# Freeing the fill of waits, reordering the half round and spreading the last picks in a convolution and expert-routing kernel

## The chip, the cores and the metric

The kernel runs on one core of one Trainium2 chip. The metric is the device time of one execution in microseconds (us), the lower the better. Each run comes with the mean granted clock of TensorE (1.0 is full speed). A run is called slow when it is over 1.5% above the fastest run of the same kernel on that chip, and slow runs are kept out of all ratios (the medians quoted are of all runs). Some of the experiments landed on two other chips, on which the kernel before took some 18% longer. They are marked, and their absolute times are never set beside those of the ordinary chips.

## The reference

Eight sequences of 3,584 rows of 192 numbers pass through a lightweight convolution (7 taps, causal, one softmaxed filter per group of 24 channels). Each row then goes to one of eight experts, the one with the largest gate logit. The expert is a two-layer network, and its result is scaled by a softmax gate and an output gate.

```python
# x: (8, 3584, 192), weight: (8, 7); cut to what matters
w = softmax(weight)                                  # per head
out = einsum('hk,bskhg->bshg', w, windows_of(x_pad)) # causal convolution
x = out.reshape(28672, 192)
logits = x @ w_gate                                  # (192, 8)
e_idx = argmax(logits, axis=1)
gate_w = softmax(logits)[arange(N), e_idx]
eom = 1 / (1 + exp(-(x @ w_output_gate)))
for e in range(8):
    mask = e_idx == e
    h = maximum(x[mask] @ w1[e], 0.0)                # 192 -> 1024
    ye = h @ w2[e]                                   # 1024 -> 192
    out[mask] = gate_w[mask, None] * eom[mask, e, None] * ye
```

## The kernel before

The 28,672 rows are cut into 16 units of 1,792. For each unit a front part and, later, an expert part run, and the two are interleaved instruction by instruction.

The front of a unit is two generators. `front_a` convolves on TensorE (8 steps), transposes (6 steps), multiplies with the gates and transposes back (2 steps). `front_b` picks the expert of each row, counts rows per expert, computes each row's position (a matmul with a triangular matrix plus one that adds the counts, called the positions matmul below), and permutes the rows into expert order by eight groups of matmuls with 0/1 masks. GpSimd then scatters each group, with computed row addresses, into a buffer in device memory that is sorted by expert.

```python
    def evac(o, i):                  # empties a "pf" accumulation buffer
        sync_flip[0] ^= 1
        if sync_flip[0] or fill[0] is not None:
            nc.scalar.copy(out=o, in_=i)
        else:
            nc.vector.tensor_copy(out=o, in_=i)
    # ... in front_b, after the positions matmul pk:
        nc.vector.tensor_tensor(out=dm[P], in0=pk[P, 0:NB * E]..., in1=msk[P], op=ALU.mult)
        nc.vector.tensor_reduce(out=pos[P], in_=dm[P], axis=AX.X, op=ALU.add)
        # dd, R, dd, dst, du: five operations that make the rows' destinations
        ...
        prep(0)                      # scaled rows and mask of the first permutation group
        prep(1)
    # ...
    def scatter(u, du, xs, i):
        i = nc.gpsimd.indirect_dma_start(out=xcg2, out_offset=...du..., in_=xs...)
        nodep(i, f"sc{u}", [f"sc{v}" for v in range(NU)] + ["load"])
```

The list at the end of `scatter` names the transfers that a scatter need not wait for. The "guards", eight writes of zero rows to the start of each expert's region, are not in it.

The expert part works on slots of 512 sorted rows. A slot has four quarters. The first layer of two quarters (`first`) and the second layer of each (`second`) surround one step of the front of unit u+2, and one of the permutation of unit u+1. Four slots, so 16 quarters, are called a half round here, since in each the slots of four of the eight experts are served.

```python
    load_w(0)
    load_w(1)
    drain(front_a(0))
    for u in range(U0 + 1):                      # the fill: units 0, 1, 2
        fa, fb = front_a(u + 1, u < U0), front_b(u)
        drain(fa, 1)
        while drain(fb, 1):
            drain(fa, 2 if u < U0 else 1)
            emit_in(len(pend))                   # scatters
        if u == 0:
            drain(fa)
            load_w(2)
            load_w(3)
            for e in range(E):                   # the guards
                i = nc.sync.dma_start(out=xcg[e * CAP:e * CAP + TT, :]..., in_=zrow)
                nodep(i, "guard", ())
        # ...
    for u in range(U0, NU):                      # the half rounds
        # ...
            for q in range(4):
                pos = 4 * k + q
                if q % 2 == 0:
                    s.first(q // 2)
                drain(fa, 1)
                if prev is not None:
                    prev.second(q)
                    emit_out()                   # scatters of results
                if pos < 8:
                    drain(fs, 1)
                elif pos < 12:
                    drain(fa, 1)
                else:
                    drain(fbn, 1)
                emit_in(len(pend))
```

In the last unit three further slots of 256 rows are chosen at run time from what is left over. These are the "picks", each a chain of some fifteen small operations on VectorE, which all stand in one block in the middle of the half round before the last unit's (561 to 570 us), where that unit's slots are loaded.

## Time and profile before

| | before |
|---|---|
| time, median of 3 | 647.33 us (646.89 to 647.94) |
| span of the profiled run | 645.5 us, clock 0.981 |
| first slot's first matmul | at 89.18 us |
| half rounds, positions matmul to positions matmul | 37.14 and 38.39 us alternating |
| positions matmul of unit 15 to the end | 101.6 us |

These lines of the page give each engine's busy time, then the granted clock in 40 slices of the span (in tenths, 9 is full), then the chain of work that ended last by engine.

```profile
PE 586.5 (91%) x4544; PEld 360.3 (56%) x4544; DVE 406.3 (63%) x1362; ACT 355.4 (55%) x586; POOL 401.5 (62%) x419
...
PEclk9999859999999999999999999999999999999997
...
PE 66%; DVE 19%; ACT 6%; DMA 4%; issue 3%; SPq 0%; POOL 0%; DVEq 0%; ACTq 0%; POOLq 0%
```

TensorE (PE) is nearly always busy, yet the last chain runs through it for 66% of the span only. In 19% VectorE (DVE) holds it up. The slices with 8 and 5, at about 65 to 97 us, are the fill's end, where TensorE also runs at a lower clock.

### The profile page before, as it was taken

The numbers are of one execution on the slowest core, as the hardware profiler recorded it, in microseconds if no ns is written. First come the engines' busy times: TensorE is split into PE (matmuls) and PEld (weight loads), VectorE is DVE, ScalarE is ACT, GpSimd is POOL, SyncE is SP. The second block draws the span as 40 slices with busy tenths as digits, with TensorE's granted clock in tenths as the row PEclk, the third lists the DMA queues.
The fourth block names the chain that finished last, engine by engine and source line by source line (L and its number), as shares of the span: only waits on it lengthen the run. The fifth ranks groups of instructions, "written<-read, shape, count | busy, mean of one in ns | idle before, by whom it ended". The sixth has DMA issues, their size and how long they took to land.

```text
span 645.5 us, 13578 instructions
## 1 busy us (share of the span) xinstructions
PE 586.5 (91%) x4544; PEld 360.3 (56%) x4544; DVE 406.3 (63%) x1362; ACT 355.4 (55%) x586; POOL 401.5 (62%) x419
## 2 busy tenths in 40 slices
PE   3998739999999999999999999999999999979993
PEld 1554415656665566656566566655566565546662
DVE  7567536584957658494775849577594956943332
ACT  1676525554665555556555555555555565656661
POOL 1362726876775756667476655756566674777773
PEclk9999859999999999999999999999999999999997
DMA  6979439994654647264553637355372525246631
GB/s 160 191 186 258 132 76 201 143 211 137 138 169 117 176 106 171 85 153 131 117 155 101 185 87 165 105 114 165 92 188 88 107 82 113 73 108 136 188 115 37
DMA packets 162569, 88.14 MB, mean 137 GB/s; under 512 B 116765, under 2 KB 153792, under 8 KB 162496
## 3 DMA queue, kind: packets, MB, share of 16 engines
q1 hardware_dynamic: 131872, 43.92, 30.3%
q0 software_dynamic: 29728, 43.30, 25.8%
q8 instruction: 36, 0.59, 0.4%
q14 instruction: 37, 0.30, 0.2%
q10 hardware_dynamic: 896, 0.03, 0.1%
HBM read 35.92 MB, written 43.06 MB: 122 GB/s over the span
## 4 chain that ended last, share of the span: by engine, by line
PE 66%; DVE 19%; ACT 6%; DMA 4%; issue 3%; SPq 0%; POOL 0%; DVEq 0%; ACTq 0%; POOLq 0%
PE pyt L655 18%; PE pp L613 13%; PE pf L290 11%; PE pp L620 8%; PE pf L444 5%; DVE ht L631 5%; PE pf L313 5%; PE pf L304 5%; ACT ht L633 4%; DVE xrow L423 2%; DVE pm L428 2%; DVE cv L280 2%; PE pf L322 2%; DMA out_dram<-y,oi 1%; DMA xt<-in_x_dram 1%
## 5 line engine op out<-in xcount | busy, mean ns | idle before, releaser
L482 POOL DMA_INDIRECT out_dram<-y,oi x246 | 245.6, 998 | 127.6 <-ACT y L661 63.4
L633 ACT ACTIVATE ht<-pp 128x1024 f16<-128x1024 f32 (+1 forms) x189 | 183.1, 1001 | 69.8 <-PE pp L620 67.0
L655 PEld LDWEIGHTS <-ht 128*128 128x128 f16 x1968 | 166.6, 98 | 58.2 <-issue 29.5
L655 PE MATMUL pyt<-wres,ht 128*128 128x192 f16 x1920 | 192.7, 246 | 1.5 <-DVE ht L631 1.5
L462 POOL DMA_INDIRECT xcg_sorted<-xs,du x128 | 131.5, 1027 | 92.2 <-DVE tk L502 22.1
L290 PE MATMUL pf<-xt,band 118*112 118x384 f32 x256 | 109.4, 523 | 19.1 <-DMA xt<-in_x_dram 10.8
L631 DVE TENSOR_SCALAR ht<-pp 128x1024 f16<-128x1024 f32 (+1 forms) x63 | 74.7, 1185 | 71.8 <-PE pp L613 71.8
L661 ACT COPY y<-pyt 128x384 f32<-128x384 f32 x123 | 59.0, 479 | 85.6 <-PE pyt L655 84.1
L613 PE MATMUL pp<-xa,wres 128*128 128x512 f16 x240 | 92.9, 387 | 9.1 <-DMA xa<-xcg_sorted 9.1
L613 PE MATMUL pp<-xb,wres 128*128 128x512 f16 x240 | 91.3, 380 | 1.2 <-DMA xb<-xcg_sorted 1.2
L620 PE MATMUL pp<-xb,wres 64*128 64x512 f16 x240 | 73.0, 383 | 1.6 <-ACT ht L633 1.2
L620 PE MATMUL pp<-xa,wres 64*128 64x512 f16 x240 | 73.0, 383 | 0.0
L444 PE MATMUL pf<-xrow,pm 112*128 112x194 f16 x512 | 65.1, 249 | 5.8 <-DVE pm L428 4.1
L613 PEld LDWEIGHTS <-wres 128*128 128x128 f16 x480 | 34.8, 97 | 60.7 <-issue 59.7
L290 PEld LDWEIGHTS pf<-xt,band 118*112 118x112 f32 x256 | 42.5, 185 | 41.6 <-DVE cv L280 11.5
L278 ACT COPY cv<-pf 112x384 f32<-112x384 f32 x80 | 38.1, 478 | 46.5 <-PE pf L290 38.6
L428 DVE TENSOR_SCALAR pm<-pos,pos 112x256 f16<-112x256 f16 x256 | 62.1, 307 | 0.0
L423 DVE TENSOR_TENSOR xrow<-cv,gs 112x384 f16<-112x384 f32 x121 | 61.9, 551 | 0.0
L444 PEld LDWEIGHTS <-pm 112*128 112x128 f16 x512 | 44.7, 98 | 15.3 <-DVE pm L428 7.7
L304 PE MATMUL pf<-identf,cv 112*128 112x112 f32 x384 | 50.7, 260 | 2.3 <-ACT tt L278 2.1
L278 ACT CAST xs<-pf 128x388 f16<-128x388 f32 x76 | 37.1, 492 | 27.5 <-PE pf L444 27.5
L304 PEld LDWEIGHTS pf<-identf,cv 112*128 112x128 f32 x384 | 40.9, 141 | 10.0 <-ACT tt L278 3.4
(139 smaller groups left out, 447.2 us busy)
## 6 DMA issues: line engine op xcount, KB each, us to landing
xt<-in_x_dram SPq DMA_DIRECT2D x8, 1344.0 KB
xt<-in_x_dram SPq DMA_DIRECT2D x8, 1260.0 KB
out_dram<-y,oi POOLq DMA_INDIRECT x246
wres<-in_moe_w_dram POOLq DMA_DIRECT2D x8, 384.0 KB
wd<-wres SPq DMA_DIRECT2D x3, 768.0 KB
wres<-in_moe_w_dram POOLq DMA_DIRECT2D x8, 256.0 KB
xcg_sorted<-xs,du POOLq DMA_INDIRECT x128
xcg_sorted<-zrow SPq DMA_DIRECT2D x8, 256.0 KB
```

The source lines that it names most:

```text
L278: nc.scalar.copy(out=o, in_=i)
L290: nc.tensor.matmul(pc[0:BT, 0:NB * GH], band[0:KI, h, :], xt[0:KI, :, h * GH:(h + 1) * GH], start=True, stop=True)
L304: nc.tensor.matmul(pt[:, j * BT:(j + 1) * BT], cvf[0:BT, m * 2 * D + i * 128:m * 2 * D + (i + 1) * 128], identf[0:BT, 0:BT], is_transpose= ...
L428: nc.vector.tensor_scalar(out=pms[i][P, l, :], in0=pos16[P], scalar1=pos[P, l * NG + i:l * NG + i + 1], scalar2=None, op0=ALU.is_equal)
L444: nc.tensor.matmul(ps[:, r * XW:(r + 1) * XW], pm[P, l, r * 128:(r + 1) * 128], xr[P, l * NG + i, :], start=(r == 0 and l == 0), stop=(r = ...
L462: i = nc.gpsimd.indirect_dma_start(out=xcg2, out_offset=bass.IndirectOffsetOnAxis(ap=du[:, i:i + 1], axis=0), in_=xs.rearrange("p r w -> p ...
L482: i = nc.gpsimd.indirect_dma_start(out=out, out_offset=bass.IndirectOffsetOnAxis(ap=oi[:, j:j + 1], axis=0), in_=y[:, j, :], in_offset=Non ...
L613: nc.tensor.matmul(pps[r][:, l, :], w[:, o2:o2 + 128], x, start=(r == 0), stop=(r == 1))
L620: nc.tensor.matmul(pps[r][:, l, :], w[p0:p0 + 64, c:c + 128], x[p0:p0 + 64], start=(r == 1), stop=(r == 0))
L631: nc.vector.tensor_relu(out=ht, in_=pps[r])
L633: nc.scalar.activation(out=ht, in_=pps[r], func=AF.Relu)
L655: nc.tensor.matmul(self.pp[:, o:o + D], self.ht[fc // 2][:, fc % 2, q * 128:(q + 1) * 128], self.w[:, w:w + D], start=(fc == 0 and q % 2 = ...
```

## The change

It has three parts. In the fill, scatters no longer wait for the guards, the weights are split into pieces that are issued between scatters, and the order of convolution and permutation steps differs. In the half rounds, the front's steps stand at other quarters, ScalarE and VectorE take fixed shares of the copies, and the destination arithmetic moves behind the first permutation mask. The picks are spread, one after each of the last unit's first three slots.

```diff
-    def load_w(e):              # four transfers of one expert
+    def w_pieces(e):            # the same four, as a list
...
+    wq = deque(p for e in range(E) for p in w_pieces(e))
+    def load_w(n):
+        while n and wq:
+            nc.gpsimd.dma_start(*wq.popleft())
+            n -= 1
...
+    evac_on = [None]
     def evac(o, i):
         sync_flip[0] ^= 1
-        if sync_flip[0] or fill[0] is not None:
+        if evac_on[0] is not None:
+            act = evac_on[0] == "act"
+        else:
+            act = sync_flip[0] or fill[0] is not None
+        if act:
...
-        dd = pr.tile(...)       # the five destination operations
-        ...
         prep(0)
+        dd = pr.tile(...)       # now between the first mask and the second
+        ...
         prep(1)
...
-        nodep(i, f"sc{u}", [f"sc{v}" for v in range(NU)] + ["load"])
+        nodep(i, f"sc{u}", [f"sc{v}" for v in range(NU)] + ["load", "guard"])
...
-            drain(fa, 2 if u < U0 else 1)
+            n += 1
+            drain(fa, 1 if u == U0 or n > 8 else 2 if n < 8 else 0)
             emit_in(len(pend))
+            if u < U0 and n > 4 and n % 2:
+                load_w(1)
...
-        if u == NU - 1:
-            for sel, bap, inv in [pick(TP // 2) for _ in range(ND)]:
-                ...
+    def load_pick():
+        sel, bap, inv = pick(TP // 2)
+        ...
...
+                if 0 <= 16 * (u - U0) + pos - 4 < 16:
+                    load_w(1)
                 if q % 2 == 0:
                     s.first(q // 2)
-                drain(fa, 1)
+                if pos in (0, 2, 4, 6, 8, 10, 12):
+                    evac_on[0] = "act" if pos < 8 else None
+                    drain(fa, 1)
+                if pos == 14:
+                    drain(fbn, 1)
                 if prev is not None:
                     prev.second(q)
                     emit_out()
+                if pos in (1, 3, 5, 7, 8, 9, 10, 11):
+                    evac_on[0] = "dve" if pos < 8 else None
+                    drain(fa, 2 if pos == 9 else 1)
                 if pos < 8:
+                    evac_on[0] = "act"
                     drain(fs, 1)
...
+                if pos == 12:
+                    drain(fbn, 1)
+                if pos == 15:
+                    drain(fbn, 2)
...
+                if u == NU - 1 and q == 3 and k < ND:
+                    todo.append(load_pick())
```

More of the change, by code (lines that the diff above doesn't have):

```diff
@@ L202 @@
     wres = const.tile([128, E * WE], FP16)
-    def load_w(e):
+    def w_pieces(e):
         o = e * WE
         w = moe_w1[e]
-        nc.gpsimd.dma_start(
-            wres[:, o:o + F].rearrange("p (l c) -> p l c", l=2),
-            bass.AP(tensor=w.tensor, offset=w.offset,
-                    ap=[[F, 128], [64 * F + F // 2, 2], [1, F // 2]]))
-        nc.gpsimd.dma_start(wres[0:64, o + F:o + WA], w[0:64, F // 2:F])
-        nc.gpsimd.dma_start(wres[64:128, o + F:o + WA], w[128:D, 0:F // 2])
-        nc.gpsimd.dma_start(
-            wres[:, o + WA:o + WE].rearrange("p (c d) -> p c d", d=D),
-            moe_w2[e].rearrange("(c p) d -> p c d", p=128))
+        return [
+            (wres[:, o:o + F].rearrange("p (l c) -> p l c", l=2),
+             bass.AP(tensor=w.tensor, offset=w.offset,
+                     ap=[[F, 128], [64 * F + F // 2, 2], [1, F // 2]])),
+            (wres[0:64, o + F:o + WA], w[0:64, F // 2:F]),
+            (wres[64:128, o + F:o + WA], w[128:D, 0:F // 2]),
+            (wres[:, o + WA:o + WE].rearrange("p (c d) -> p c d", d=D),
+             moe_w2[e].rearrange("(c p) d -> p c d", p=128))]
+    wq = deque(p for e in range(E) for p in w_pieces(e))
[3 more added lines that the diff above has]
+            n -= 1
     GE = NG * E
@@ L393, in front_b @@
         nc.vector.tensor_reduce(out=pos[P], in_=dm[P], axis=AX.X, op=ALU.add)
-        dd = pr.tile([128, NG, E + 1], FP32, tag="dd", name="dd")
-        nc.vector.tensor_tensor(
-            out=dd, in0=pk[:, c0 + NSEG:c0 + 2 * NSEG].rearrange("p (i e) -> p i e", e=E + 1),
-            in1=bass.AP(tensor=R9.tensor, offset=R9.offset,
-                        ap=[list(R9.ap[0]), [0, NG], [1, E + 1]]), op=ALU.add)
-        nc.vector.tensor_tensor(out=R, in0=R, in1=pk[:, c0 + 2 * NSEG:NK], op=ALU.add)
-        nc.vector.scalar_tensor_tensor(
-            out=dd, in0=pk[:, c0:c0 + NSEG].rearrange("p (i e) -> p i e", e=E + 1),
-            scalar=rowf[:, 0:1], in1=dd, op0=ALU.is_le, op1=ALU.mult)
-        dst = pr.tile([128, NG], FP32, tag="dst", name="dst")
-        nc.vector.tensor_reduce(out=dst, in_=dd, axis=AX.X, op=ALU.max)
-        du = pr.tile([128, NG], U32, tag="du", name="du")
-        nc.vector.tensor_scalar(out=du, in0=dst, scalar1=rowf[:, 0:1], scalar2=None, op0=ALU.add)
         xr = xrows[u % 2]
@@ L432, in front_b @@
         prep(0)
+        dd = pr.tile([128, NG, E + 1], FP32, tag="dd", name="dd")
+        nc.vector.tensor_tensor(
+            out=dd, in0=pk[:, c0 + NSEG:c0 + 2 * NSEG].rearrange("p (i e) -> p i e", e=E + 1),
+            in1=bass.AP(tensor=R9.tensor, offset=R9.offset,
+                        ap=[list(R9.ap[0]), [0, NG], [1, E + 1]]), op=ALU.add)
+        nc.vector.tensor_tensor(out=R, in0=R, in1=pk[:, c0 + 2 * NSEG:NK], op=ALU.add)
+        nc.vector.scalar_tensor_tensor(
+            out=dd, in0=pk[:, c0:c0 + NSEG].rearrange("p (i e) -> p i e", e=E + 1),
+            scalar=rowf[:, 0:1], in1=dd, op0=ALU.is_le, op1=ALU.mult)
+        dst = pr.tile([128, NG], FP32, tag="dst", name="dst")
+        nc.vector.tensor_reduce(out=dst, in_=dd, axis=AX.X, op=ALU.max)
+        du = pr.tile([128, NG], U32, tag="du", name="du")
+        nc.vector.tensor_scalar(out=du, in0=dst, scalar1=rowf[:, 0:1], scalar2=None, op0=ALU.add)
         prep(1)
@@ L682, in chain @@
             yield from g
-    load_w(0)
-    load_w(1)
+    load_w(8)
     drain(front_a(0))
@@ L690 @@
         drain(fa, 1)
+        n = 0
         while drain(fb, 1):
-            drain(fa, 2 if u < U0 else 1)
+            n += 1
+            drain(fa, 1 if u == U0 or n > 8 else 2 if n < 8 else 0)
             emit_in(len(pend))
+            if u < U0 and n > 4 and n % 2:
+                load_w(1)
+        if u < U0:
+            drain(fa)
         if u == 0:
-            drain(fa)
-            load_w(2)
-            load_w(3)
             for e in range(E):
                 i = nc.sync.dma_start(
-                    out=xcg[e * CAP:e * CAP + TT, :].rearrange("(p g) w -> p (g w)", g=GR), in_=zrow)
+                    out=xcg[e * CAP:e * CAP + TT, :].rearrange("(p g) w -> p (g w)", g=GR),
+                    in_=zrow)
                 nodep(i, "guard", ())
-        elif u < U0:
-            drain(fa)
     def loads(u):
@@ L709, in loads @@
             todo.append((wres[:, e * WE:(e + 1) * WE], inv, slot_load(base, u)))
-        if u == NU - 1:
-            for sel, bap, inv in [pick(TP // 2) for _ in range(ND)]:
-                base = reg(bap[0:1, 0:1], [ET.SP], E * CAP - TT)
-                todo.append((w_dyn(sel), inv, slot_load(base, u, TT // 2)))
-        return todo
+        return todo
+    def load_pick():
+        sel, bap, inv = pick(TP // 2)
+        base = reg(bap[0:1, 0:1], [ET.SP], E * CAP - TT)
+        return w_dyn(sel), inv, slot_load(base, NU - 1, TT // 2)
     todo = loads(U0)
@@ L729 @@
             fa, fbn = front_a(u + 2), front_b(u + 2)
-        nxt = None
-        for k, (w, inv, xabi) in enumerate(todo):
-            if 0 < 4 * (u - U0) + k <= EH:
-                load_w(EH - 1 + 4 * (u - U0) + k)
+        k = 0
+        while k < len(todo):
+            w, inv, xabi = todo[k]
             s = Slot(xabi, w, inv)
@@ L742 @@
                     emit_out()
+                if pos in (1, 3, 5, 7, 8, 9, 10, 11):
+                    evac_on[0] = "dve" if pos < 8 else None
+                    drain(fa, 2 if pos == 9 else 1)
                 if pos < 8:
+                    evac_on[0] = "act"
                     drain(fs, 1)
-                elif pos < 12:
-                    drain(fa, 1)
-                else:
+                    evac_on[0] = None
+                    emit_in(len(pend))
+                if pos == 12:
                     drain(fbn, 1)
-                emit_in(len(pend))
+                if pos == 15:
+                    drain(fbn, 2)
                 if pos == 7 and u + 1 < NU:
                     nxt = loads(u + 1)
+                if u == NU - 1 and q == 3 and k < ND:
+                    todo.append(load_pick())
             prev = s
+            k += 1
         todo = nxt
```

## The prediction

> **What bounds the kernel now.** I read the page first, for the stages, then the timelines of the engines in each stage. TensorE is busy 91% of the span and carries 66% of the chain of waits, so a gain has to come out of TensorE's idle time or its slow clock. There are three places: the fill (0 to 89 us), the steady half rounds, and the tail. The fill first: TensorE's timeline (start, us, engine, line, tiles, idle before and what ended it).
>
> ```profile
> 80.34 0.23 PE L386 MATMUL pf<-lsum,np 64*128 64x152 f16 x1
> 89.18 0.59 PE L613 MATMUL pp<-xa,wres 128*128 128x512 f16 x1 [8.61 <-DMA xa<-xcg_sorted]
> 90.51 0.59 PE L613 MATMUL pp<-xb,wres 128*128 128x512 f16 x1 [0.74 <-DMA xb<-xcg_sorted]
> ...
> 97.09 0.38 PE L613 MATMUL pp<-xb,wres 128*128 128x512 f16 x1
> ```
>
> The first slot's matmuls wait 8.61 us for their rows, then run at 0.59 us instead of 0.38. The rows are loaded only when the last scatter of unit 2 has landed, so GpSimd's timeline tells why they are late:
>
> ```profile
> 49.74 0.98 POOL L213 DMA_DIRECT2D wres<-in_moe_w_dram  x1
> 63.26 1.05 POOL L462 DMA_INDIRECT xcg_sorted<-xs,du  x1 [12.54 <-DVE du L407]
> 64.61 1.38 POOL L462 DMA_INDIRECT xcg_sorted<-xs,du  x1 [0.30 <-issue]
> ...
> 83.83 0.98 POOL L462 DMA_INDIRECT xcg_sorted<-xs,du  x1 [0.31 <-issue]
> ```
>
> GpSimd stands idle for 12.54 us with unit 1's first tile ready since 49.7 (its copy on ScalarE starts at 49.18 and takes 0.50), then issues 16 scatters back to back, one per 1.29 us. The releaser named, du, is unlikely: unit 1's du was written at 47.30. In the instruction order of the kernel before, this scatter also waits on all eight hardware queues, which are the guard writes (issued from 46.78 to 53.84). I take the guards for the cause.
>
> The steady half round: TensorE's waits over two half rounds (196.57 to 272.11 us), then where they lie in the first of them.
>
> ```profile
> PE pf L290 <- DVE cv L280: 1.1, 2, 0.7
> PE pf L313 <- DVE tt L280: 0.4, 1, 0.4
> PE pf L304 <- ACT tt L278: 0.3, 1, 0.3
> ```
>
> ```profile
> 213.53 0.90 PE L290 MATMUL pf<-xt,band 118*112 118x384 f32 x2 [0.74 <-DVE cv L280]
> ...
> 233.14 1.71 PE L313 MATMUL pf<-tt,wg 128*32 128x448 f32 x16 [0.41 <-DVE tt L280]
> ```
>
> These show only 1.8 us of 75.5, because short waits vanish under the modelled ends of matmuls. Start-to-start times show more. Unstalled pieces are: two quarters of a slot 2.83 us (598.97 to 601.80, first and second layer), a convolution step 0.65, a transpose step 0.39, the gate matmuls 1.65, their transposes 0.48, a permutation group 0.335, the counts 0.15 and the positions 0.40. A half round is 8x2.83 + 8x0.65 + 6x0.39 + 1.65 + 0.48 + 8x0.335 + 0.55 = 35.5 us. The trace has 75.54/2 = 37.77. So 2.25 us per half round is waiting, nearly all for the two "pf" buffers to be emptied. At 212.93 VectorE empties one that was full since about 211.8 (its matmuls start at 210.98 and take 0.81), because a 1.22 us relu and the 1.41 us plan stand before it in its queue:
>
> ```profile
> 211.31 0.17 DVE L518 TENSOR_SCALAR iu<-iv 128x16 uint32<-128x16 f32 x1
> 211.40 0.48 DVE L428 TENSOR_SCALAR pm<-pos,pos 112x256 f16<-112x256 f16 x2
> 211.79 1.22 DVE L631 TENSOR_SCALAR ht<-pp 128x1024 f16<-128x1024 f32 x1
> 212.93 0.55 DVE L280 COPY cv<-pf 112x384 f32<-112x384 f32 x1
> ```
>
> The tail: TensorE waits 1.52 us at 571.39 for VectorE, which works at the three picks from 561.37 to 569.64. But GpSimd issues without a break from 553.52 to the end:
>
> ```profile
> 634.62 0.48 ACT L661 COPY y<-pyt 128x384 f32<-128x384 f32 x1 [1.60 <-PE pyt L655]
> 635.40 0.98 POOL L482 DMA_INDIRECT out_dram<-y,oi  x1 [0.30 <-ACT y L661]
> 636.69 0.99 POOL L482 DMA_INDIRECT out_dram<-y,oi  x1 [0.31 <-DVEq L774]
> ```
>
> **What the Trainium skill says.** "Perfetto Trace Analysis", DMA Instruction — SWDGE: the recorded end of a GpSimd DMA is the end of descriptor generation, not of the transfer. The trace agrees: the last scatter before the first slot takes 0.98 us on GpSimd, and the chain then has 2.38 us for it as a DMA. "TensorE: Matmul & The Clock Gate", What's actually happening: an idle window of about 3.4 us halves the clock, and busy time restores it. The trace agrees: 0.59 against 0.38 us after 8.61 us of idling, and a granted clock of 0.58 from 80 to 90 us. "Perfetto Trace Analysis", Consistent bubbles under Optimization Strategy: a gap that repeats can mean too few buffers for the next tile. Here it is two "pf" buffers and a late reader. "DMA: Bandwidth & Descriptors", Issuing engines are not separate DMA queues: transfers of all engines share the same 16 DMA engines. From 50 to 64 us this trace has a DMA share of 1.15 to 1.32 and 235 to 308 GB/s, so guards, weights and input do compete there.
>
> **The change, part by part.** 1. *Fill.* No instruction is added; scatters lose the wait for the guards, and weights 2 and 3 go as eight pieces between scatters. GpSimd's new schedule: unit 0 starts at 33.54 as before and has 8x1.29 + 2.9 (four pieces, 0.77+0.60+0.58+0.97) = 13.2 us, to 46.7. Unit 1 starts when its first tile is ready, some 48.7 (below), and takes 13.2, to 61.9. Unit 2's first tile was ready at 65.4 and comes about 3 us earlier, at 62.4; its eight scatters end at 62.4 + 8x1.29 = 72.7, against 84.8. Landing and load follow as before: first transfer issued 1.8 us after that end (84.8 to 86.6), matmul 2.6 later, so at about 77.1.
> TensorE's own path to that point: the gate transposes of a unit move behind its fifth permutation group, and the destination arithmetic (five operations, 1.06 us, 204.28 to 205.34) moves behind the first permutation mask. That removes most of two waits of 0.98 us (40.79, 57.22) and 1.1 of the 1.80 at 64.10. So 80.5 becomes about 77.4. Both chains meet near 77.4; with a wait for xb I say 78. Gain 89.2 - 78 = 11 us. The clock: the first block, from 90.51, loses about 2.4 us at 0.59 us per matmul to 96.5; an idle gap of at most 2.1 us (before 79.38) should save half or more of it. Fill: **12.5 us**.
>
> 2. *Half rounds.* Copies of convolutions alternate ScalarE (before the second layer) and VectorE (after it), all row copies go to ScalarE. VectorE loses on average 4x0.55 us, ScalarE gains 4x0.48 and has room (55% busy). Two users of "pf" no longer stand a second layer apart in the same order, and the gate transposes wait over a first layer (1.51 us) instead of a second (0.66). But the counts move from the 14th quarter to the 15th and the positions from the 15th to the end of the 16th, behind a relu on VectorE. By hand, with the durations above: positions wait 0.3 for the counts, the first permutation group 0.2 for its mask, the convolution in quarter 3 0.3 for its buffer, the gate 0.2: 1.0 us left of 2.25. Gain 1.25, taken as 1.1 for waits I did not see, in 11 half rounds (units 3 to 13) and a little in unit 2: **13 us**.
>
> 3. *Picks.* They leave VectorE's busy stretch (3x2.7 us at 561 to 570), so the waits of 1.18 and 1.52 us go. Yet the first load of the next slots is issued at 572.27, after GpSimd's last scatter (569.45), and GpSimd has some 65 issues ((637.7 - 553.5) / 1.29) of 1.29 us in a row to the end. TensorE will wait for the load instead: **0 to 1 us**.
>
> Sum: 12.5 + 13 + 0.5 = 26 us; 647.3 - 26 = 621.
>
> **Rivals.** (a) VectorE becomes the bound at the edge of half rounds: its queue from the 15th quarter through the 4th has some 15 us of work against 15 us of TensorE's, so my 1.0 us could be 2 and the gain near 3 us in all: about 632. For it: positions are later. Against: VectorE does 2.2 us less per half round. (b) In the fill DMA is the bound: the same 7 MB go through a stretch already at a share above 1, and a scatter waits for its queue's transfer eight issues back; then unit 2 ends only some 5 us earlier: about 628. Against: weights start at 34, where DMA was not full (0.55 from 40 to 50). (c) GpSimd limits the half round: 16 issues of 1.29 us in the first eight quarters are 20.6 us, and TensorE without waits needs 19.2. It recovers in the last eight (10.3 of 16.3), so I give this nothing, apart from the tail. (d) All waits of the half round vanish: 25 instead of 13, about 609.
>
> **Range and chances.** (a) and (b) together give some 639, (d) alone 609; both ends are unlikely. 611 to 632 should hold it 8 times in 10. 2% is 634.4: faster 0.93, same 0.06, slower 0.01.
>
> **What would show it.** First slot's matmul at 76 to 80 us instead of 89.18, no gap near 12 us on GpSimd before unit 1, scatters with weight pieces between them from 34 to 62. Two half rounds in 72 to 74 us instead of 75.5, with fewer waits of convolutions for VectorE and new ones of the positions or first masks. From unit 14's first quarter to the end about 100 us as before (544.7 to 645.5), with a longer wait for xa. It is wrong if the first slot still starts after 84, if two half rounds take over 75, or if the tail gains over 2 us.

## The result, and the profile after

| | before | after | difference |
|---|---|---|---|
| time, median of 4 runs each | 647.11 us | 623.82 us (622.84 to 624.0) | -23.3 |
| span of the profiled run | 645.5 us | 621.1 us | -24.4 |
| clock | 0.981 | 0.985 | |
| first slot's first matmul | 89.18 | 78.23 | -10.95 |
| from there to the positions matmul of unit 15 | 454.7 | 441.0 | -13.7 |
| from there to the end | 101.6 | 101.9 | +0.3 |

The ratio is 0.9636 (95% interval 0.9619 to 0.9652), so faster. Ratios are the mean time of one kernel's fast runs over that of the other's of the same rounds, so not quite the ratio of the quoted medians. The three stages add up to the whole. The same lines of the page as before:

```profile
PE 575.6 (93%) x4544; PEld 359.2 (58%) x4544; DVE 380.4 (61%) x1310; ACT 381.8 (61%) x638; POOL 403.5 (65%) x419
...
PEclk9999989999999999999999999999999999989997
...
PE 80%; DVE 7%; ACT 5%; DMA 4%; issue 2%; POOL 1%; ACTq 0%; SPq 0%; POOLq 0%; DVEq 0%
```

VectorE's share of the last chain fell from 19% to 7%, and the work moved to ScalarE shows as 52 instructions more there and 52 fewer on VectorE. The reader should also see a new 8 near the end of the clock's row. It will matter.

**The fill.** GpSimd's timeline after, at unit 1's first scatters and the last two of unit 2 (start, us, engine, line, operation, tiles, idle before and its releaser):

```profile
47.45 1.21 POOL L475 DMA_INDIRECT xcg_sorted<-xs,du  x1 [1.04 <-ACT xs L291]
48.65 1.15 POOL L221 DMA_DIRECT2D wres<-in_moe_w_dram  x1
...
71.57 0.98 POOL L475 DMA_INDIRECT xcg_sorted<-xs,du  x1 [0.72 <-DMA xcg_sorted<-xs,du]
72.86 0.98 POOL L475 DMA_INDIRECT xcg_sorted<-xs,du  x1 [0.30 <-DVE mx L351]
```

The gap of 12.54 us is gone. The first scatter of unit 1 starts at 47.45 instead of 63.26, right after its rows are ready, and a weight piece follows it. The guards are still issued (from 50.15 us), but nothing waits for them. TensorE's timeline in the same stretch:

```profile
74.91 0.23 PE L399 MATMUL pf<-lsum,np 64*128 64x152 f16 x1
78.23 0.59 PE L626 MATMUL pp<-xa,wres 128*128 128x512 f16 x1 [3.10 <-DMA xa<-xcg_sorted]
79.41 0.59 PE L626 MATMUL pp<-xb,wres 128*128 128x512 f16 x1 [0.59 <-DMA xb<-xcg_sorted]
...
84.52 0.50 PE L457 MATMUL pf<-xrow,pm 112*128 112x194 f16 x4
84.85 0.38 PE L626 MATMUL pp<-xa,wres 128*128 128x512 f16 x1
```

TensorE now waits 3.10 us for the rows instead of 8.61, but its first matmuls still run at 0.59 us. Between its first xb matmul and the first one at 0.38 us lie 5.44 us (79.41 to 84.85); before, the same instructions took 6.36 us (90.51 to 96.87), 0.37 us of the difference being a shorter wait for a copy. So about 0.5 us of clock was saved. This profiled run has the earliest first slot of all. Two experiments below with the very same fill code, on an ordinary chip, have it at 78.71 and 79.86 us, so the 10.95 us of the table is good to a microsecond or so.

**The half rounds.** TensorE's waits from 112 to 520 us (what waited, what ended it, us in all, times, longest), before and then after:

```profile
PE pf L290 <- DVE cv L280: 6.6, 12, 0.7
PE pf L304 <- ACT tt L278: 2.1, 6, 0.4
PE pf L313 <- DVE tt L280: 2.1, 5, 0.4
```

```profile
PE pf L457 <- ACT cv L291: 4.0, 10, 0.4
PE pf L398 <- DVE og L384: 3.1, 10, 0.3
PE pp L626 <- DMA xb<-xcg_sorted: 0.6, 1, 0.6
PE pf L457 <- DVE pm L427: 0.4, 1, 0.4
PE pf L398 <- DVE np L382: 0.3, 1, 0.3
```

None of the three old waits (convolutions for VectorE, transposes, gate) is left. Two new ones come once in each half round: 0.3 us of the positions matmul (L398) and 0.4 us of the first permutation group (L457). The half rounds became even, 36.67 us each, so that two take 73.33 us instead of 75.53.

The two new waits, in the timelines of one half-round edge: TensorE, then VectorE, then ScalarE.

```profile
189.14 0.23 PE L398 MATMUL pf<-lsum,np 64*128 64x128 f16 x1 [0.32 <-DVE og L384]
...
192.75 0.49 PE L457 MATMUL pf<-xrow,pm 112*128 112x194 f16 x4 [0.40 <-ACT cv L291]
```

```profile
187.20 1.23 DVE L644 TENSOR_SCALAR ht<-pp 128x1024 f16<-128x1024 f32 x1 [0.44 <-PE pp L626]
188.34 0.14 DVE L377 TENSOR_SCALAR nu<-pf 64x1 uint32<-64x1 f32 x1
188.51 0.14 DVE L379 TENSOR_SCALAR nu<-nu 64x1 uint32<-64x1 uint32 x1
188.69 0.39 DVE L382 CAST np<-nu 64x128 f16<-64x128 uint32 x1
...
191.58 0.47 DVE L427 TENSOR_SCALAR pm<-pos,pos 112x256 f16<-112x256 f16 x2
```

```profile
190.40 1.94 ACT L646 ACTIVATE ht<-pp 128x1024 f16<-128x1024 f32 x2 [0.35 <-PE pp L633]
192.22 0.48 ACT L291 COPY cv<-pf 112x384 f32<-112x384 f32 x1
```

The counts were on TensorE at 187.09, but VectorE could turn them into np only after a relu of 1.23 us; np is ready at about 189.1, and the positions matmul waits. (The view names og, which runs next, as releaser; by order of data it is np.) The first permutation group is not late because of its mask, which is ready at about 192.05. It waits until 192.70 for ScalarE's copy of the convolution, which stands behind two relus: in the built program (not in a trace) the group's accumulation buffer is the one that this convolution used.

**The tail.** From unit 15's positions matmul (543.86 us before, 519.21 after) TensorE waits as follows, for the picks and at the first load of the last slots, before and then after:

```profile
571.39 1.00 PE L655 MATMUL pyt<-wres,ht 128*128 128x192 f16 x10 [1.52 <-DVE ht L631]
...
576.57 0.38 PE L613 MATMUL pp<-xb,wres 128*128 128x512 f16 x1 [0.48 <-DMA xb<-xcg_sorted]
```

```profile
548.95 0.39 PE L626 MATMUL pp<-xa,wres 128*128 128x512 f16 x1 [1.73 <-DMA xa<-xcg_sorted]
550.31 0.38 PE L626 MATMUL pp<-xb,wres 128*128 128x512 f16 x1 [0.97 <-DMA xb<-xcg_sorted]
...
552.29 2.41 PE L668 MATMUL pyt<-wres,ht 128*128 128x192 f16 x16
```

The 16 second-layer matmuls at 552.29 take 2.41 us instead of 1.48 (as at 545.73). This is the 8 in the clock's row. Measured in parts, the tail is: positions matmul to this xb matmul 31.10 us (before 32.71, where it started at 576.57), from there to the last copy of a result 59.67 us (before 58.05), from there to the end 11.12 us (before 10.88). So spreading the picks did gain 1.6 us up to the load, and a slower clock took the same back.

That the clock fell here is not a fixed consequence of the waits. The experiment "The weights in one lump" below has the same code from the half rounds to the end, and in its trace:

```profile
560.27 0.39 PE L626 MATMUL pp<-xa,wres 128*128 128x512 f16 x1 [1.96 <-DMA xa<-xcg_sorted]
561.47 0.38 PE L626 MATMUL pp<-xb,wres 128*128 128x512 f16 x1 [0.81 <-DMA xb<-xcg_sorted]
...
562.76 1.48 PE L668 MATMUL pyt<-wres,ht 128*128 128x192 f16 x16
```

TensorE waits as long (2.77 us in all, against 2.70), but the 16 matmuls take 1.48 us and the granted clock of the ten microseconds after is 1.00. The three parts are 31.17, 58.04 and 11.09 us, so that tail takes 100.3 us and gains 1.3 over the kernel before.

### The profile page after: what moved, and what is told of

It reads as the page before. It is cut to its first block, busy times and chain, and to the rows that moved or that the text cites.

```text
span 621.1 us, 13578 instructions
## 1 busy us (share of the span) xinstructions
PE 575.6 (93%) x4544; PEld 359.2 (58%) x4544; DVE 380.4 (61%) x1310; ACT 381.8 (61%) x638; POOL 403.5 (65%) x419
## 4 chain that ended last, share of the span: by engine, by line
PE 80%; DVE 7%; ACT 5%; DMA 4%; issue 2%; POOL 1%; ACTq 0%; SPq 0%; POOLq 0%; DVEq 0%
PE pyt L668 22%; PE pp L626 18%; PE pf L303 12%; PE pp L633 10%; PE pf L457 6%; PE pf L317 6%; PE pf L326 4%; ACT ht L646 3%; DVE ht L644 2%; PE pf L335 1%; ACT cv L291 1%; DMA out_dram<-y,oi 1%; DMA xb<-xcg_sorted 1%; DVE np L382 1%; DVE xrow L422 1%
## 5 line engine op out<-in xcount | busy, mean ns | idle before, releaser
L668 PEld LDWEIGHTS <-ht 128*128 128x128 f16 x1968 | 167.4, 98 | 24.4 <-issue 10.9
L475 POOL DMA_INDIRECT xcg_sorted<-xs,du x128 | 133.3, 1042 | 72.4 <-ACT xs L291 31.7
L303 PE MATMUL pf<-xt,band 118*112 118x384 f32 x256 | 104.9, 504 | 11.0 <-DMA wg<-n_moe_w_output_gate_dram 10.6
L291 ACT CAST xs<-pf 128x388 f16<-128x388 f32 x128 | 61.6, 485 | 49.7 <-PE pf L457 47.9
L457 PE MATMUL pf<-xrow,pm 112*128 112x194 f16 x512 | 64.5, 247 | 7.4 <-ACT cv L291 4.0
L457 PEld LDWEIGHTS <-pm 112*128 112x128 f16 x512 | 44.9, 97 | 34.5 <-issue 12.3
L293 DVE COPY cv<-pf 112x384 f32<-112x384 f32 x48 | 26.5, 551 | 42.9 <-PE pf L303 42.8
L317 PE MATMUL pf<-identf,cv 112*128 112x112 f32 x384 | 49.3, 259 | 0.7 <-ACT cv L291 0.7
```

The lines of the kernel that those rows point to most:

```text
L303: nc.tensor.matmul(pc[0:BT, 0:NB * GH], band[0:KI, h, :], xt[0:KI, :, h * GH:(h + 1) * GH], start=True, stop=True)
L317: nc.tensor.matmul(pt[:, j * BT:(j + 1) * BT], cvf[0:BT, m * 2 * D + i * 128:m * 2 * D + (i + 1) * 128], identf[0:BT, 0:BT], is_transpose= ...
L457: nc.tensor.matmul(ps[:, r * XW:(r + 1) * XW], pm[P, l, r * 128:(r + 1) * 128], xr[P, l * NG + i, :], start=(r == 0 and l == 0), stop=(r = ...
L475: i = nc.gpsimd.indirect_dma_start(out=xcg2, out_offset=bass.IndirectOffsetOnAxis(ap=du[:, i:i + 1], axis=0), in_=xs.rearrange("p r w -> p ...
L668: nc.tensor.matmul(self.pp[:, o:o + D], self.ht[fc // 2][:, fc % 2, q * 128:(q + 1) * 128], self.w[:, w:w + D], start=(fc == 0 and q % 2 = ...
```

## The experiments

Twelve runs of nine kernels were made, in three lots. The first and the third lot landed on two chips where the kernel before took 761.43 and 762.8 us (medians of 23 and 7 executions), at clocks of 0.92 to 0.94. There the intervals are two to six times as wide as the result's above, and steady half rounds vary between 41 and 52 us (42.2 to 51.6 within one run). The kernel before and the change itself have no trace from these chips. From those only stage lengths and the presence of single waits are read, next to the ratios. All kernels but one gave correct results.

### The fill alone

```diff
 # the kernel before, with the change's w_pieces, fill loop and
-        nodep(i, f"sc{u}", [...] + ["load"])
+        nodep(i, f"sc{u}", [...] + ["load", "guard"])
 # half rounds, copies, destination arithmetic and picks as before
```

First run, on the first slower chip:

> The fill part alone on the kernel before (no wait for guards, weight pieces, step counts of the fill; destination arithmetic not moved). My theory: the first slot's matmul comes at 79 to 80 us instead of 89.18 and nothing after it changes, so 9 to 10.5 us are gained: ratio 0.984 to 0.986. Rival (the gain of the fill is given back because the half rounds absorb it): under 5 us, ratio above 0.992.

Measured: 746.94 us median against 761.43, but three of four runs were slow, so no ratio came out. The first slot in the profiled (slow) run started at 79.11. Inconclusive on the time.

Again, on the second slower one:

> The fill alone (as the first run of it, on a chip at its ordinary clock). Theory that the parts are independent: the first convolution of the units' loop starts near 79 us instead of 89.2, the half rounds stay at 38.4 and 37.1 alternating, the tail at 101.6; 9 to 10.5 us gained, ratio 0.984 to 0.986. Rival, that the fill only pays together with the new half rounds (later waits give it back): under 6 us, ratio above 0.991.

Measured: 751.08 us against 762.8, ratio 0.9769 [0.9667, 0.9871]. The first slot started at 80.73, so the fill is shortened without any of the other parts. The interval contains the theory's 0.984 to 0.986 and leaves out the rival's 0.991.

### The half round alone

```diff
 # the kernel before, with the change's half-round loop, evac_on and place of dd;
 # fill, whole-expert weight loads and picks as before
+                if 0 < 4 * (u - U0) + k <= EH:
+                    load_w(EH - 1 + 4 * (u - U0) + k)
-                if 0 <= 16 * (u - U0) + pos - 4 < 16:
-                    load_w(1)
```

The lines shown are the difference from the changed kernel's loop.

> The order of the half rounds and the engines of the copies alone, with the destination arithmetic moved; fill, weights and picks as before. My theory: 11 half rounds of 36.7 instead of 37.8 us, 12 to 14 us, ratio 0.978 to 0.982. Rival (the half rounds gained only because the fill had put weights and scatters elsewhere): under 8 us, ratio above 0.988.

Measured on the first slower chip: 739.47 us, ratio 0.9735 [0.9627, 0.9842].

> The reordered half round alone. Theory: the first slot stays near 89 us, the half rounds become even at 36.7 us, 12 to 14 us gained, ratio 0.978 to 0.982. Rival, that the finer weight pieces share in it: the half rounds stay above 37.2 and under 8 us are gained, ratio above 0.988. With the fill alone it should add up to the whole change, 0.9636.

Measured on the second: 741.24 us, ratio 0.9706 [0.9642, 0.977]. The expected 0.978 to 0.982 lies just outside this interval and inside the first, and the expected length of 36.7 us could not be seen on chips with half rounds of 41 to 48 us. That this part gains without the new fill and its weight pieces is clear from both: the rival's 0.988 is excluded twice.

### The picks alone

```diff
 # the kernel before, with the change's load_pick and
+                if u == NU - 1 and q == 3 and k < ND:
+                    todo.append(load_pick())
```

> The spread picks alone. My theory: GpSimd paces the tail, so TensorE waits longer for its rows in place of the two waits for VectorE, and the time is the same within 1 us: ratio 0.9985 to 1.0015. Rival (TensorE paces the tail): the 2.7 us of the two waits are gained, ratio 0.996.

Measured on the first slower chip, 20 executions: 760.62 us, ratio 0.9984 [0.9949, 1.0019].

> The spread picks alone. Theory that the issues of GpSimd set the tail, whatever VectorE's waits: no change, ratio 0.9985 to 1.0015. Rival, that the picks' waits were on the path: 2 us or more gained, ratio under 0.997.

Measured on the second, 4 executions: 753.35 us, ratio 0.9874 [0.9806, 0.9942]. The two contradict each other. On the first, nothing; on the second, 1.3%. For the change itself there are the two tails above, 0.3 us longer with the slower clock and 1.3 us shorter without it; what the picks alone would give on an ordinary chip stays open.

The stages of the profiled runs on the second slower chip tell where each part acts, better than the ratios do:

| kernel | first slot at | to unit 15's positions | to the end |
|---|---|---|---|
| fill alone | 80.73 | 542.2 | 126.5 |
| half round alone | 93.27 | 523.4 | 122.7 |
| picks alone | 88.36 | 534.8 | 121.5 |
| whole change, with one relu moved (below) | 79.57 | 520.1 | 122.9 |

The first column is short with the new fill only, the second with the new half round only. So the two parts act in separate stages. (Single traces scatter: the picks alone, which touch neither, had 92.44 and 542.3 on the first slower chip.) The three ratios do not add to the whole on that chip (11.72 + 21.56 + 9.45 = 42.7 us from the medians, against 38.0 for the last row's kernel, which has all three), which at such scatter says nothing about the parts' independence.

### The guards alone

```diff
 # the changed kernel
-        nodep(i, f"sc{u}", [...] + ["load", "guard"])
+        nodep(i, f"sc{u}", [...] + ["load"])
```

> The changed kernel with its scatters waiting for the guard writes again. If the guards are the cause of the 12.5 us gap on GpSimd, unit 1's first scatter moves from 47.45 to about 63 to 65, unit 2's last from 73.8 to about 85 to 89 (12 scatters or so and four pieces remain), the first slot to about 90, and 10 to 14 us are lost: 634 to 638 us. If du or the data were the cause, nothing changes: 624.

Measured on the first slower chip: 732.29 us, ratio 0.9663 [0.9572, 0.9753]. The trace shows the effect in its place. GpSimd, with the last scatter of unit 0 and the first of unit 1:

```profile
46.59 1.01 POOL L475 DMA_INDIRECT xcg_sorted<-xs,du  x1 [0.30 <-ACT cv L291]
59.37 0.99 POOL L475 DMA_INDIRECT xcg_sorted<-xs,du  x1 [11.76 <-DVE dm L402]
```

The wait for the guards alone restores the gap (11.76 us, 12.54 before) and puts the first slot's matmul back to 88.58 us, although everything else of the new fill is kept (the fill alone, with the guards freed, had it at 79.11 on this same chip):

```profile
88.58 0.58 PE L626 MATMUL pp<-xa,wres 128*128 128x512 f16 x1 [11.34 <-DMA xa<-xcg_sorted]
```

The guards are the cause, as the prediction took them to be; the releaser that the view names was wrong here as it was before. The ratio cannot be set against the changed kernel's, which did not run on that chip.

### The destination arithmetic alone

```diff
 # the changed kernel
+        dd = pr.tile(...)       # the five operations back, ahead of xr and prep(0)
         xr = xrows[u % 2]
```

> The changed kernel with the five operations of the destination arithmetic back in front of the first mask. Theory one (the mask is what the first permutation group waits for): the mask comes 1.06 us later, after 192.9 instead of 191.98 in the half round I read, the group some 0.3 us later than now in each of 12 half rounds, 2 to 5 us lost with the fill's 1 us. Theory two (the group waits for its accumulation buffer, emptied by ScalarE at 192.70, so the mask is hidden): under 1 us lost per run.

Measured on an ordinary chip, 5 rounds: 628.16 us, ratio 0.9698 [0.9669, 0.9726], against 0.9636 for the whole change: some 4 us lost, as theory one expected. Half rounds of 37.05 us instead of 36.67, and the first slot at 78.93. TensorE's waits from 112 to 520 us:

```profile
PE pf L456 <- DVE pm L440: 7.7, 11, 1.2
PE pf L398 <- DVE og L384: 3.3, 10, 0.4
```

Now the first permutation group waits 0.65 us for its mask instead of 0.40 us for a buffer. So the move is worth 0.38 us per half round, some 4 us in eleven, less than the arithmetic's own time of 1.06 us, since a second wait stood behind the first. In the fill it is worth less still: the kernel without the move has no wait of TensorE between 36 and 61 us, where the kernel before had two of 0.98, so the new order of gate and permutation steps removed those, and the move only split a wait of unit 2 (one of 1.65 us without it; 0.60, 0.48 and 0.28 with it).

### The copies alone

```diff
 # the changed kernel: copies alternate between ScalarE and VectorE again
-        if evac_on[0] is not None:
+        if False:
```

> The changed kernel with every copy of the half rounds alternating between the two engines again, the order of steps kept. If the fixed engines are worth something, VectorE, which takes four more row copies of 0.55 us in half of the half rounds, delays buffers: 0.3 to 1 us per half round, 4 to 10 us lost. If the order alone made the gain: within 1.5 us.

Measured on the same ordinary chip, 3 rounds: 635.16 us, ratio 0.9807 [0.9775, 0.984]. The half rounds alternate again, 38.13 and 36.97 us, 37.55 on average. Waits of TensorE from 112 to 520 us:

```profile
PE pf L457 <- ACT cv L291: 7.1, 14, 0.6
PE pf L398 <- DVE og L384: 3.5, 11, 0.3
PE pf L457 <- DVE dd L439: 2.2, 6, 0.7
```

The fixed shares are worth 0.88 us per half round (37.55 - 36.67) and are the largest single piece of that part; the new order and the moved arithmetic without them leave only 0.2 us of gain (37.77 to 37.55). The 11.3 us lost are more than the 4 to 10 expected; in this trace the tail too is 1.7 us longer. Together with the 0.38 us of the arithmetic the shares are 1.26 us, more than the 1.10 that the half round gained as a whole: the pieces overlap, probably since removing either leaves the other's wait to show.

### The weights in one lump

```diff
 # the changed kernel
-            if u < U0 and n > 4 and n % 2:
-                load_w(1)
         if u == 0:
+            load_w(8)
```

> The changed kernel with the eight pieces of weights 2 and 3 in one lump after unit 0's scatters. My theory: the pieces cost GpSimd the same 5.5 us in either place and unit 2's scatters end with their data, so unit 2's last scatter moves by less than 1 us and the time is the same within 1 us. Rival: the lump pushes unit 1's scatters back by 2.8 us and with them the row buffers of unit 2, and 1 to 3 us are lost.

Measured on the same chip, 5 rounds: 628.05 us (625.93 to 632.32), ratio 0.9704 [0.9671, 0.9737]. GpSimd in the fill:

```profile
45.64 5.54 POOL L221 DMA_DIRECT2D wres<-in_moe_w_dram  x8
...
58.82 0.98 POOL L475 DMA_INDIRECT xcg_sorted<-xs,du  x1 [3.67 <-DMA wres<-in_moe_w_dram]
61.45 0.98 POOL L475 DMA_INDIRECT xcg_sorted<-xs,du  x1 [1.65 <-DMA wres<-in_moe_w_dram]
```

Eight pieces in a row cost GpSimd 5.54 us, and later scatters wait 3.67 and 1.65 us for weight transfers. The first slot starts at 83.84 instead of 78.23. In the profiled run, the slowest of the six, one later load of rows also came 2.81 us late and cost a half round of 42.82 us with a clock of 0.66 for ten of them. So spreading the pieces is worth 5.6 us in the fill of this trace, and without it freeing the guards would have gained about half of the 11 us there. By the medians the lump costs 4.2 us in all (628.05 against 623.82). Both expectations missed: within 1 us, and the rival's 1 to 3. What they left out are the scatters' waits for weight transfers.

### Fewer result scatters in the tail (wrong on purpose)

```diff
 # the changed kernel; the results of every fourth quarter of the last two units stay out
-                pout.extend((self.y, self.oi, j) for j in (q - 1, q))
+                pout.extend((self.y, self.oi, j) for j in (q - 1, q)
+                            if not (self.short and j == 3))
...
             s = Slot(xabi, w, inv)
+            s.short = u >= NU - 2
```

> Wrong result on purpose: the last of four output scatters of each full slot of units 14 and 15 is left out, 12 issues of 1.29 us in all. If GpSimd's issues pace the tail, up to 15.4 us less, and some 8 to 12 because TensorE becomes the limit before that. If TensorE paces the tail: under 2 us less.

Measured on the same chip, 3 rounds: 619.61 us, ratio 0.9582 [0.9541, 0.9624]. The result is wrong (missing rows). With 12 scatters fewer (234 instead of 246; 12 x 1.29 = 15.5 us of GpSimd's time) the tail took 96.6 us instead of 101.9. By the parts of the tail named above: 29.78 us to the xb matmul (31.10), 58.05 to the last copy (59.67), 8.71 to the end (11.12). The middle part is the clock's (58.04 also in the run with the lump, at full clock), which leaves 3.7 us for the issues. So GpSimd's backlog holds up the load and the last results, but each issue costs far less than its own length. Neither expectation was met: by the medians 4.2 us were gained, fewer than 8 to 12 and more than 2. The ten microseconds that begin around that load, as a window (stretch, its length, busy us of TensorE, its weight loads, VectorE, ScalarE and GpSimd, then the granted clock, the DMA share and GB/s), first of the changed kernel, then of this one:

```profile
549.20:559.20 10.00, 9.03 (x60) 4.98 (x59) 2.71 (x12) 4.84 (x6) 7.30 (x8) 0.83 0.67 132
```

```profile
551.40:561.40 10.00, 10.00 (x85) 6.04 (x85) 4.21 (x20) 7.31 (x9) 5.14 (x6) 1.00 0.68 128
```

After waits of 0.85 and 0.54 us the clock stayed at 1.00; after 1.73 and 0.97 us it fell to 0.83, as it did after 2.21 and 1.00 in the run with the arithmetic moved back. This is the clock that cancelled the picks' gain. But after 1.96 and 0.81 us, in the run with the lump, it stayed at 1.00, so these traces give no length of wait from which it falls.

### One relu moved to ScalarE

```diff
 # the changed kernel: the relu ahead of the counts runs on ScalarE
-        def first(self, q2):
+        def first(self, q2, act=False):
...
-                if q == 3:
+                if q == 3 and not act:
...
-                    s.first(q // 2)
+                    s.first(q // 2, pos == 14)
```

> The changed kernel with one relu per half round (the one ahead of the counts) moved from VectorE to ScalarE. Theory that the wait of the positions' matmul (0.32 us) is VectorE's: that wait goes, half rounds 36.3 to 36.4 instead of 36.67, 3 to 7 us less than the changed kernel, ratio 0.953 to 0.959. Rival, that ScalarE, which already empties the bank that the first group of permutation matmuls waits for, then holds that group longer: the 0.40 us wait grows by what the other loses or more, within 1.5 us of the changed kernel or slower, ratio 0.961 to 0.972.

Measured on the second slower chip: 724.85 us (724.36 to 725.81), ratio 0.9488 [0.9427, 0.9548]. A positions matmul and the first permutation group after it:

```profile
342.04 0.23 PE L398 MATMUL pf<-lsum,np 64*128 64x128 f16 x1
...
345.71 0.51 PE L457 MATMUL pf<-xrow,pm 112*128 112x194 f16 x4 [0.46 <-DVE dd L434]
```

The wait of the positions matmul is gone in all half rounds, and so is the one on ScalarE's copy; eight waits on VectorE, 0.56 us on average, stand at permutation groups instead. So the positions' wait was VectorE's relu. The rival's worry about ScalarE is not settled: in the built program the edit also gave the first permutation group the other accumulation buffer, the one that the destination arithmetic reads last, so that it no longer waits for ScalarE at all. And in this trace ten convolutions wait 33.0 us in all for a copy on ScalarE, where the run with the guards back, on the other slower chip, has seven such waits of 20.8 us; whether the edit or the chip made the difference is not shown. Whether it beats the changed kernel stays open: that one did not run on this chip, half rounds there vary more than the 0.3 us in question, and another kernel on the first slower chip, without this edit, had a middle stage as short (518.2 us against 520.1).

## Why the prediction was right, point by point

The time was 623.82 us against 621.0 predicted, inside the range of 611 to 632, and faster, to which 0.93 was given.

**Fill: 12.5 us predicted, 11.45 shown** (10.95 up to the first slot and 0.5 of clock). The removed wait was the right one, as the run with the guards back shows. The first slot was put at 78 and came at 78.23, which is partly luck. The scatters end at 73.84 us instead of the predicted 72.7, for two of unit 2's take 1.34 and 1.42 us and one waits 0.72. (The trace before had such long ones too: its 16 scatters, read as one per 1.29 us, stand 1.37 apart on average.) From there on the transfer is issued 1.79 us later and the matmul 2.60 later, as the prediction had read them off the trace before. TensorE's own path, on the other hand, was ready at 75.1 instead of 77.4; about 1 us of this is the very start, where the same 16 convolutions took 7.53 us instead of 8.36 and began 0.2 us earlier. No edit explains that; in the four ordinary-chip experiments, which start with the same code, they took 8.11 to 8.54 us, so it is the luck of this run. So the step "both chains meet near 77.4" failed: the scatter chain alone set the time, TensorE idled 3.1 us instead of at most 2.1, the clock stayed low, and the 1.2 us or more of clock came out as 0.5. The mechanism was right, and this term was mis-sized. The 0.6 us added for xb, on which this matmul does not wait, made up for part of the late scatters.

**Half rounds: 13 us predicted, 13.2 measured** (13.7 for the stage, less the 0.5 of clock counted in the fill). From unit 4's positions matmul (127.76 us before, 115.09 after) to unit 15's, eleven half rounds gained 11.98 us, 1.09 each where 1.1 was taken; the stretch from the first slot to unit 4's positions gave the remaining 1.7, so 1.2 without the clock, where the prediction's "little in unit 2" was 0.9. Against 35.5 us of work without waits, 36.67 leaves 1.17 us where the hand count had 1.0. Of its four waits, the positions' (0.3) is there at 0.32 and has the predicted cause. The first permutation group (0.2) waits 0.40, for a buffer on ScalarE and not for its mask. The convolution in quarter 3 (0.3) and the gate (0.2) show no wait in the view. The sum was right while its parts were partly wrong.

**Picks: 0 to 1 us predicted, -0.3 measured.** As predicted, VectorE's long waits went and a longer wait for xa came. What was left out is that this wait can slow the clock. In this trace that cost 1.6 us and took back the 1.6 gained; in the trace with the lump it did not happen and the tail gained 1.3 us, so which of the two a run shows is chance. The prediction's reason, that GpSimd has its issues in a row, holds in part. Its "without a break" was read too broadly: after 553.52 us GpSimd stood idle 2.03 us once and about 0.5 five times. Fewer issues shorten the tail, but by 5.3 us, 1.6 of it clock, for 15.5 us of issues.

**Rivals.** VectorE as the bound at the edge (a) appears only as the positions' 0.32 us: 1.17 us of waiting is left per half round, not 2. DMA in the fill (b) is not the bound in the changed kernel, though it becomes one when the weights go in a lump. GpSimd in the half round (c) left no wait of TensorE for rows in the steady rounds beyond 0.6 us once. That all waits vanish (d) did not happen, since each removed wait had a smaller one behind it.

The sum of 26 us was 1.6 too high against the 24.4 of the profiled runs: 1.05 in the fill and 0.8 in the picks, less 0.2 the other way in the half rounds. The profiled run was the fastest of the four; the medians differ by 23.3 us.

## What to carry to other kernels

Follow a long gap of an issuing engine back to what its instruction really waits for, in the order of the program and not only in the name that a view gives: waiting for eight writes that nothing needed yet cost most of the fill's 11 us, though only with the weights spread as well. When a wait is removed, look for the next one behind it at the same place, because the gain is the difference of the two; this made 1.06 us of moved arithmetic worth 0.38. Give copies to engines by their place in the round rather than in turn. Read the granted clock after an idle stretch in several runs: here 2.7 us of waiting slowed it in one trace and 2.8 us did not in another.

## What the Trainium skill lacked or had wrong

- "DMA: Bandwidth & Descriptors", Anatomy of one DMA — SWDGE (gpsimd) path, calls descriptor generation "small, variable" in a fixed cost of about 2 us. For the indirect scatters here it is not small: GpSimd is held 0.98 us by 279 of the changed kernel's 374 (1.81 at most) and can start the next 0.30 us later, a rhythm of 1.29 us. 374 x 1.29 = 482 us of a span of 621. (The same page's latency table does count about 1 us of emission, which fits; the rhythm of one issue after another I found on no page.)
- "TensorE: Matmul & The Clock Gate", What's actually happening, speaks of an idle window of about 3.4 us. Here shorter waits slowed the matmuls too: after 3.10 us they ran at 0.59 instead of 0.38 us, and after 1.73 and 0.97 us, 0.4 us of work between them, the clock of the next ten microseconds was 0.83. After 1.96 and 0.81 us, in another run with the same code there, it stayed at 1.00, and so after 0.85 and 0.54 us. So no length of a wait alone decides. That the window runs freely, as the page says, may explain it; no run here shows the window.
- I found no page on chips on which one and the same kernel takes longer by so much: 761.43 and 762.8 us against 647.11 for the kernel before, with clocks of 0.92 to 0.94. The clock is not the whole of it. In the second run of the picks alone, on such a chip, a first-layer matmul took 401 ns on average instead of the 386 of the kernel before, 4% more, from 200 to 480 us, but 102 instead of 119 of them were done, 14% fewer, with waits spread over all engines. Its cause stays open.
